# A diagonal of reciprocals as the moving operand of the transposes, in a two-precision attention and feed-forward kernel

## The chip, the cores and the metric

One Trainium2 chip, one core of it. The metric is device time in microseconds (us) of one execution. The kernel before took 974.97 us, the median of 3 runs that lie between 972.93 and 976.83.

## The reference

Windowed attention with global tokens for 4 batches of 8 heads, 512 local and 32 global positions, head dimension 64, then two feed-forward blocks on the 2176 rows of 512 that come out. Cut to what matters:

```
s = concat(scale * q_l @ k_g.T, where(|i - j| <= 32, scale * q_l @ k_l.T, -1e9))
e = exp(s - max(s))
out_l = (e / (sum(e) + 1e-9)) @ concat(v_g, v_l)
out_g = softmax(scale * q_g @ concat(k_g, k_l).T) @ concat(v_g, v_l)
x = rows of (out_g, out_l)
x = (silu(x @ w_gate) * (x @ w_val)) @ w_out          # 512 -> 1536 -> 512
h = x @ w_in                                          # 512 -> 2048 -> 512
y = (max(h, 0) + alpha * min(h, 0)) @ w_out2
```

The changed lines compute `e / (sum(e) + 1e-9)`, in the form that the product with v needs: turned, with the keys on the partitions.

## The kernel before, in words

The feed-forward products are what most of the time goes into. Each weight and each activation is held as a rounded 32-bit value and its rest, and a product is three matmuls (`passes`, line 495: high by high, high by low, low by high). `mm12` (line 502) makes one 128-row piece of a hidden layer from 12 matmuls, `down` the product back to 512 rows. `visit1` is one pass of the first block over some columns of one batch, `visit2` one of the second block.

Attention is cut into units. A `Local` unit is one pair of heads and one half (256) of the positions of one batch, in five steps: `s` (line 164) makes the scores in PSUM (8 matmuls, of which the profile shows two records for each program instruction), masks them and finds the row minimum of the negated scores on VectorE (line 184), and takes the exponential with its row sum on ScalarE (line 197). `n` (line 202) adds 1e-9 to the sums, takes the reciprocals `rc`, and multiplies each of four 128 by 256 blocks of `e` by its column of `rc` (line 207). `t` (line 215) is called twice, once per head: it turns the 128 by 512 probabilities with four TensorE transposes against the identity (line 229) into one PSUM bank, which ScalarE copies to `pt` (line 154). `pv` (line 232) multiplies `pt` with v (line 250) and writes the result to `xa` or `yp`. Batches 2 and 3 (`SPLIT`, line 29) take another way: `n` scales `e` by a power of two as well, and `t` makes two 16-bit parts of it which a DMA turns. Batches 0 and 1 have 16 of the 32 local units, so 64 of the 128 multiplications of line 207 and all 128 transposes of line 229. `Global` units (lines 267 to 336) have steps of the same names and are not touched.

`apump` (line 359) calls one step of three neighbouring units at a time; `pumper` hands such steps out between the pieces of a visit. First come the opening steps of batch 0, with nothing but weight loads beside them (the loop at line 688), then `visit1` runs while the attention of later batches is mixed in. Weights come from DRAM as 64-bit words and are turned to 32 bits on ScalarE and VectorE (`wpump`, line 437) in the same in-order queues. The order on each engine is made when the program is built: the framework's scheduler takes the calls with their priorities and its own estimates of times, so that a change to one step can move others. Buffers of `e`, `pt`, `rc` come from the pool `attp` with two buffers each.

Of the kernel before, what the change touches and what calls it, by code (L numbers as in the profile page):

```python
# [10 lines left out]
F32 = mybir.dt.float32  # L11
# [7 lines left out]
ALU = mybir.AluOpType  # L19
# [8 lines left out]
PSC = 32768.0  # L28
# [14 lines left out]
def kernel(  # L43
# [11 lines left out]
    nc = tc.nc  # L55
# [25 lines left out]
    attp = tc.alloc_tile_pool(name="attp", bufs=2, side="right", reuse_waits="tile")  # L81

    ident = const.tile([128, 128], F32, name="ident")
# [19 lines left out]
    def att_bank():  # L103
        t = att_tags["list"][att_tags["i"] % len(att_tags["list"])]
        att_tags["i"] += 1
        return bank(t)
# [4 lines left out]
    def heat(n):  # L111
        t = bank("g")
        for _ in range(n):
            nc.tensor.matmul(out=t[:, 0:128], lhsT=zero, rhs=zero, start=True, stop=True)
# [35 lines left out]
    def evac(out, in_, name):  # L150
        if frac(name):
            nc.vector.tensor_copy(out, in_)
        else:
            nc.scalar.activation(out=out, in_=in_, func=ACTF.Copy)
# [4 lines left out]
    class Local(Unit):  # L159
# [42 lines left out]
        def n(self):  # L202
            rc = attp.tile([128, 4], F32, tag="rc", name="rc")
            nc.vector.tensor_scalar(out=rc, in0=self.sm, scalar1=1e-9, scalar2=None, op0=ALU.add)
            nc.vector.reciprocal(out=rc, in_=rc)
            for j in range(4):
                nc.vector.tensor_scalar(
                    out=self.e[:, j], in0=self.e[:, j], scalar1=rc[:, j:j + 1],
                    scalar2=PSC if self.split else None, op0=ALU.mult,
                    op1=ALU.mult if self.split else ALU.bypass,  # L210
                )
            if self.split and self.half == 0:
                self.pair.split_v()

        def t(self, h):
            src = self.e[:, 2 * h:2 * h + 2].rearrange("p a b -> p (a b)")
            if self.split:
                if h == 0:
                    self.pt = attp.tile([128, 2, 8, 128], F16, tag="pt", name="pth")
                p = attp.tile([128, 2, 512], F16, tag="p", name="p", bufs=3)  # L220
                nc.scalar.activation(out=p[:, 0], in_=src, func=ACTF.Copy)
                nc.vector.tensor_tensor(out=p[:, 1], in0=src, in1=p[:, 0], op=ALU.subtract)
                nc.sync.dma_start_transpose(out=self.pt[:, h], in_=p.rearrange("p a b -> p (a b)"))
                return
            if h == 0:
                self.pt = attp.tile([128, 2, 512], F32, tag="pt", name="pt")
            t = att_bank()
            for i in range(0, 512, 128):
                nc.tensor.transpose(t[:, i:i + 128], src[:, i:i + 128], ident)  # L229
            evac(self.pt[:, h], t, "cp0" if st["k"] < mark[0] + LAG else "cp1")  # L230

        def pv(self):
# [118 lines left out]
    def later(n, f):  # L351
        due.setdefault(st["k"] + n, []).append(f)
# [72 lines left out]
    def wlow():  # L425
        while wlo and wlo[0][3] <= st["w"] - P["wd"]:
            key, raw, t, _, z = wlo.popleft()
            with pr("hilo"):
                eng = nc.gpsimd if frac("lo" + z) else nc.vector
                eng.tensor_tensor(out=t[:, 1], in0=raw, in1=t[:, 0], op=ALU.subtract)  # L430
            wt[key] = t
            if key[0] == 1:
                i = "gvo".index(key[2])
                with pr("st"):
                    (nc.scalar if P["q_st"] else nc.sync).dma_start(out=w1s[key[1]][:, i], in_=t.bitcast(F32))

    def wpump():
# [21 lines left out]
        for key, raw, pool, _ in ready:  # L459
            t = pool.tile([128, 2, 512], F32R, tag="w", name="w")  # L460
            z = "0" if st["k"] < mark[1] else "1" if st["k"] < mark[2] else "3" if key[0] == 2 else "2"
            with pr("hilo"):
                if frac("hi" + z):
                    nc.vector.tensor_copy(t[:, 0], raw)
                else:
                    nc.scalar.activation(out=t[:, 0], in_=raw, func=ACTF.Copy)
            wlo.append((key, raw, t, st["w"], z))
# [386 lines left out]
```

## Time and profile before

| what | value |
|---|---|
| median of 3 runs | 974.97 us |
| the profiled execution | 976.99 us |
| its span, first to last instruction | 975.2 us |
| mean granted TensorE clock | 0.983 of 2.4 GHz |
| instructions in the trace | 14802 |

The profiled execution is a separate one, 2.0 us above the median of the runs. Its span is 1.8 us shorter than its time; the rest lies around the first and the last instruction. The page of the profile gives busy time of each engine, a picture of the span in 40 slices, the chain of work that ended last, and groups of instructions by line. PE is TensorE's matmuls, PEld its weight loads, DVE is VectorE, ACT is ScalarE. A busy time of PE counts a matmul from its start to its modelled end, and matmuls overlap, so the distance between two starts, and not the duration, is what one of them costs in a row of them.

### The profile page before, as it was taken

The page shows a single profiled execution, that of the slowest core. Times are in us where ns is not written, and L with a number is a line of the kernel's source. Part 1 is how long each engine was busy: PE and PEld are TensorE (multiplying, and loading weights), DVE is VectorE, ACT ScalarE, POOL GpSimd, SP SyncE. Part 2 cuts the span into 40 slices and gives each one's busy share as a digit, 9 for nine tenths or more (in the row PEclk, how much of TensorE's full clock was granted, in tenths as well). Part 3 has the DMA queues.
Part 4 walks back from the last instruction along what each step waited for, and adds up shares of the span by engine and source line. Part 5 has one row for each costly group of instructions (what it writes and reads, how often), then busy time and mean ns, then how long its engine had stood idle before and what let it go on. Part 6 is the DMA issues. An engine that isn't in the chain of part 4 may idle for free.

```text
span 975.2 us, 14802 instructions
## 1 busy us (share of the span) xinstructions
PE 957.0 (98%) x5716; PEld 798.1 (82%) x5716; DVE 553.1 (57%) x1295; ACT 488.7 (50%) x983; POOL 0.7 (0%) x6
## 2 busy tenths in 40 slices
PE   8799999999999999999999999999999999999998
PEld 5577887777777777778999998888888888899897
DVE  5989888774444564426831289834443543544453
ACT  6888999865665666635532256423222322322322
POOL 0000000000000000000000000000000000000000
PEclk7599999999999999999999999999999999999999
DMA  8879795538662466712477043200000100010000
GB/s 263 289 244 333 249 346 183 197 85 238 170 157 73 71 153 172 174 23 87 127 215 221 1 131 115 79 1 21 23 1 0 44 1 1 1 44 1 13 21 22
DMA packets 67478, 111.86 MB, mean 115 GB/s; under 512 B 37712, under 2 KB 41808, under 8 KB 67408
## 3 DMA queue, kind: packets, MB, share of 16 engines
q1 hardware_dynamic: 67408, 110.92, 37.1%
q8 instruction: 45, 0.74, 0.3%
q14 instruction: 25, 0.20, 0.1%
HBM read 79.18 MB, written 23.33 MB: 105 GB/s over the span
## 4 chain that ended last, share of the span: by engine, by line
PE 89%; ACT 5%; DVE 4%; DMA 1%; issue 1%; SPq 1%; ACTq 0%
PE ps_acc L632 19%; PE ps_g L508 18%; PE ps_v L508 18%; PE ps_acc L541 13%; PE ps_a L508 10%; PE ps_a L171 3%; PE ps_a L241 2%; ACT e L197 1%; DMA dbl<-in_w_dram 1%; PE ps_a L250 1%; PE ps_a L282 1%; PE ps_a L229 1%; PE ps_a L325 1%; DVE w L430 1%; PE ps_acc L250 1%
## 5 line engine op out<-in xcount | busy, mean ns | idle before, releaser
L508 PE MATMUL ps_g<-xa,w 128*128 128x512 f32 (+2 forms) x1032 | 209.4, 351 | 0.4 <-ACT sg L555 0.4
L508 PE MATMUL ps_v<-xa,w 128*128 128x512 f32 (+2 forms) x1032 | 207.2, 349 | 0.5 <-DVE w L430 0.5
L508 PEld LDWEIGHTS ps_g<-xa,w 128*128 128x128 f32 x1032 | 169.5, 190 | 29.5 <-issue 7.5
L508 PEld LDWEIGHTS ps_v<-xa,w 128*128 128x128 f32 x1032 | 170.1, 190 | 25.3 <-issue 4.2
L632 PE MATMUL ps_acc<-w,h 128*128 128x512 f32 x561 | 138.3, 392 | 0.0
L632 PEld LDWEIGHTS ps_acc<-w,h 128*128 128x128 f32 x561 | 104.5, 188 | 22.3 <-DVE h L651 0.5
L541 PE MATMUL ps_acc<-h,w 128*128 128x512 f32 (+2 forms) x600 | 119.0, 350 | 0.2 <-DVE h L572 0.2
L541 PEld LDWEIGHTS ps_acc<-h,w 128*128 128x128 f32 x600 | 97.7, 189 | 15.4 <-issue 2.4
L508 PE MATMUL ps_a<-xa,w 128*128 128x512 f32 (+2 forms) x480 | 100.8, 359 | 0.0
L508 PEld LDWEIGHTS ps_a<-xa,w 128*128 128x128 f32 x480 | 83.5, 188 | 13.4
L564 DVE TENSOR_TENSOR t<-ps_v,sg 128x512 f32<-128x512 f32 (+1 forms) x54 | 35.6, 659 | 94.2 <-PE ps_v L508 82.4
L197 ACT ACTIVATE e<-e,mx 128x256 f32<-128x256 f32 x128 | 63.7, 500 | 10.6 <-DVE mx L184 9.7
L650 ACT ACTIVATE h<-g 128x512 fp32r<-128x512 f32 (+2 forms) x55 | 31.2, 568 | 74.4 <-DVE g L649 74.4
L184 DVE CUSTOM_DVE_ANT_0 e<-ps_a,lm 128x256 f32<-128x256 f32 x112 | 41.5, 419 | 44.8 <-PE ps_a L171 44.4
L632 PE MATMUL ps_acc<-w,hx 128*128 128x512 f32 x255 | 63.1, 394 | 0.0
L646 DVE TENSOR_SCALAR g<-ps_a,alpha 128x512 f32<-128x512 f32 (+2 forms) x40 | 26.8, 670 | 57.3 <-ACT r L645 56.8
L632 PEld LDWEIGHTS ps_acc<-w,hx 128*128 128x128 f32 x255 | 47.5, 188 | 10.4
L555 ACT ACTIVATE sg<-ps_g 128x512 f32<-128x512 f32 (+1 forms) x54 | 30.9, 573 | 47.2 <-PE ps_g L508 46.8
L651 DVE TENSOR_TENSOR h<-g,h 128x512 fp32r<-128x512 f32 (+2 forms) x55 | 33.6, 612 | 31.1 <-ACT h L650 31.0
L645 ACT ACTIVATE r<-ps_a 128x512 f32<-128x512 f32 (+2 forms) x40 | 21.2, 530 | 58.7 <-PE ps_a L508 58.3
L649 DVE TENSOR_TENSOR g<-g,r 128x512 f32<-128x512 f32 (+2 forms) x80 | 48.8, 611 | 2.4
L555 ACT ACT_TABLE_LOAD x30 | 38.5, 1283 | 19.4 <-PE ps_g L508 19.0
(133 smaller groups left out, 1124.1 us busy)
## 6 DMA issues: line engine op xcount, KB each, us to landing
w<-w1s SPq DMA_DIRECT2D x54, 512.0 KB, 4.1
dbl<-in_w_dram SPq DMA_DIRECT2D x50, 512.0 KB, 4.0
w1s<-w SPq DMA_DIRECT2D x36, 512.0 KB, 4.9
qk<-in_qk_dram SPq DMA_DIRECT2D x12, 592.0 KB, 5.2
dblx<-in_w_dram SPq DMA_DIRECT2D x9, 512.0 KB, 6.1
yp<-in_w_dram SPq DMA_DIRECT2D x9, 512.0 KB, 5.8
out_dram<-o SPq DMA_DIRECT2D x16, 256.0 KB, 2.1
v<-in_v_dram SPq DMA_DIRECT2D x12, 320.0 KB, 3.7
```

The source lines that it names most:

```text
L171: nc.tensor.matmul(out=s[h][:, 256 * i:256 * i + 256], lhsT=x[rows, WIN + 128 * t:WIN + 128 * t + 128], rhs=x[rows, 128 * t:128 * t + 256] ...
L184: nc.vector.tensor_tensor_reduce(out=self.e[:, j], in0=s[h][:, 256 * i:256 * i + 256], in1=lm[:, 2 * self.half + i], scale=-0.125, scalar= ...
L197: nc.scalar.activation(out=self.e[:, j], in_=self.e[:, j], func=ACTF.Exp, scale=-1.0, bias=mx[:, j:j + 1], accum_out=self.sm[:, j:j + 1],)
L508: nc.tensor.matmul(out=o, lhsT=a, rhs=x, start=(i == 0), stop=(i == 11))
L541: nc.tensor.matmul(out=acc[m][:, 0:n], lhsT=a, rhs=x, start=(f == fs[0] and j == 0), stop=(f == fs[-1] and j == 2),)
L555: nc.scalar.activation(out=sg[:, 0:nn], in_=g[:, 0:nn], func=ACTF.Silu)
L564: nc.vector.tensor_tensor(out=t[:, 0:nn], in0=v[:, 0:nn], in1=sg[:, 0:nn], op=ALU.mult)
L632: nc.tensor.matmul(out=acc[t], lhsT=a, rhs=x, start=(i == 0 and j == 0), stop=(i == NF2 - 1 and j == 2))
L646: nc.vector.tensor_scalar(out=g[:, 0:n], in0=u[:, 0:n], scalar1=0.0, scalar2=alpha[:, f:f + 1], op0=ALU.min, op1=ALU.mult)
L649: nc.vector.tensor_tensor(out=g[:, 0:n], in0=g[:, 0:n], in1=r[:, 0:n], op=ALU.add)
L650: nc.scalar.activation(out=h[:, 0, 0:n], in_=g[:, 0:n], func=ACTF.Copy)
L651: nc.vector.tensor_tensor(out=h[:, 1, 0:n], in0=g[:, 0:n], in1=h[:, 0, 0:n], op=ALU.subtract)
```

## The change

For batches 0 and 1 (units that are not `split`), `n` no longer multiplies `e`. It makes four 128 by 128 tiles `d`, the identity with each row multiplied by that row's reciprocal. `t` multiplies by `d` with ordinary matmuls where it had transposes against the identity: the stationary operand is the same block of `e`, the moving operand is now `d`, and the sum over the rows leaves e turned, with each column already divided. The block of `d` is chosen by head and 128-row tile (`2 * h + i // 2`). The split units keep the old way.

```
@@ n
+            if not self.split:
+                self.d = attp.tile([128, 4, 128], F32, tag="d", name="d")
+                for j in range(4):
+                    nc.vector.tensor_scalar(
+                        out=self.d[:, j], in0=ident, scalar1=rc[:, j:j + 1], scalar2=None, op0=ALU.mult
+                    )
+                return
             for j in range(4):
                 nc.vector.tensor_scalar(
-                    out=self.e[:, j], in0=self.e[:, j], scalar1=rc[:, j:j + 1],
-                    scalar2=PSC if self.split else None, op0=ALU.mult,
-                    op1=ALU.mult if self.split else ALU.bypass,
+                    out=self.e[:, j], in0=self.e[:, j], scalar1=rc[:, j:j + 1], scalar2=PSC, op0=ALU.mult,
+                    op1=ALU.mult,
                 )
@@ t
-            for i in range(0, 512, 128):
-                nc.tensor.transpose(t[:, i:i + 128], src[:, i:i + 128], ident)
+            for i in range(4):
+                nc.tensor.matmul(
+                    out=t[:, 128 * i:128 * i + 128], lhsT=src[:, 128 * i:128 * i + 128],
+                    rhs=self.d[:, 2 * h + i // 2], start=True, stop=True,
+                )
```

The scheduler also orders instructions of the first two batches anew. On TensorE, behind the first scores of batch 0 (`ps_acc_220` and the like are PSUM banks, `qk` holds queries and keys, and line 250 of before is line 259 now, 229 is 235), this stood before:

```order
L171 MATMUL ps_acc_328<-qk 128x256 x2
L229 MATMUL ps_acc_220<-ident,e 128x128 x4
L229 MATMUL ps_acc_233<-ident,e 128x128 x4
L250 MATMUL ps_acc_308<-pt,v 64x256
L171 MATMUL ps_acc_329<-qk 128x256
L229 MATMUL ps_a_280<-ident,e 128x128 x2
L171 MATMUL ps_acc_329<-qk 128x256
L250 MATMUL ps_acc_308<-pt,v 64x256
```

and this stands there now:

```order
L171 MATMUL ps_acc_331<-qk 128x256 x2
L235 MATMUL ps_acc_221<-d,e 128x128 x4
L235 MATMUL ps_acc_234<-d,e 128x128 x4
L235 MATMUL ps_a_282<-d,e 128x128 x4
L259 MATMUL ps_acc_311<-pt,v 64x256
L235 MATMUL ps_a_295<-d,e 128x128 x2
L171 MATMUL ps_acc_332<-qk 128x256 x2
L259 MATMUL ps_acc_311<-pt,v 64x256
```

The first head of the second unit has all its four products ahead of the first unit's product with v; before, it had two behind it, and two further on.

On TensorE just ahead of the first visit's matmuls (line 508 before, 517 now) this stood before:

```order
L250 MATMUL ps_a_509<-pt,v 64x256 x2
L250 MATMUL ps_a_509<-pt,v 64x128 x4
L229 MATMUL ps_v<-ident,e 128x128 x4
L229 MATMUL ps_a_492<-ident,e 128x128 x4
L508 MATMUL ps_v<-xa,w 128x256 x9
```

and now:

```order
L259 MATMUL ps_a_515<-pt,v 64x256 x2
L259 MATMUL ps_a_515<-pt,v 64x128 x4
L235 MATMUL ps_v<-d,e 128x128 x4
L235 MATMUL ps_a_497<-d,e 128x128 x4
L517 MATMUL ps_v<-xa,w 128x256 x6
```

Nothing has moved there but the visit's matmuls, which are broken off after 6 instead of 9 by scores of a global unit. On VectorE, at the second unit's `n` (`raw` and `dbl` are weights on their way to 32 bits), this stood before:

```order
L207 TENSOR_SCALAR e<-e,rc 128x256 x4
L184 ISA e,mx<-ps_g,lm 128x256
L184 ISA mx 128x1
L204 TENSOR_SCALAR rc<-sm 128x4
L184 ISA e,mx<-ps_v,lm 128x256
L184 ISA mx 128x1
L451 TENSOR_SCALAR raw<-raw 128x512
L205 RECIPROCAL rc<-rc 128x4
```

and now:

```order
L209 TENSOR_SCALAR d<-ident,rc 128x128 x4
L204 TENSOR_SCALAR rc<-sm 128x4
L205 RECIPROCAL rc<-rc 128x4
L209 TENSOR_SCALAR d<-ident,rc 128x128
L460 TENSOR_SCALAR raw<-raw 128x512
L209 TENSOR_SCALAR d<-ident,rc 128x128
```

The masking of the fourth unit's scores (`ps_g`, `ps_v`) has gone behind the second unit's diagonals and the first weights. On SyncE's queue some twenty transfers of the first two batches change places with a neighbour; the first of them is a second store of a turned weight (line 435, now 444), which goes ahead of the two loads of queries and keys that stood before it.

## Rows read from the trace of the kernel before

**Rows 1.** The page's picture in 40 slices: TensorE and its granted clock, in tenths.

```profile
PE   8799999999999999999999999999999999999998
...
PEclk7599999999999999999999999999999999999999
```

**Rows 2.** Windows of the whole core: stretch, us, busy us and instructions by engine, clock, DMA.

```profile
0.00:48.00 48.00, 38.14 (x176) 27.37 (x176) 35.30 (x121) 34.83 (x89) 0.70 (x6) 0.68 0.86 276
48.00:140.00 92.00, 88.90 (x751) 75.06 (x751) 80.80 (x224) 84.83 (x176) 0.00 (x0) 1.00 0.83 288
140.00:182.00 42.00, 42.00 (x264) 30.91 (x264) 36.71 (x104) 39.69 (x82) 0.00 (x0) 1.00 0.65 228
...
80.00:100.00 20.00, 19.23 (x168) 16.19 (x168) 19.35 (x59) 18.02 (x40) 0.00 (x0) 1.00 0.93 338
100.00:120.00 20.00, 19.57 (x169) 17.25 (x172) 16.18 (x43) 19.91 (x45) 0.00 (x0) 1.00 0.77 260
```

**Rows 3.** Windows of line 229 alone: stretch, us, PE busy (records), PEld busy, clock, DMA.

```profile
13.90:34.20 20.30, 4.20 (x16) 3.00 (x16) 0.50 0.88 288
34.40:37.70 3.30, 1.09 (x8) 0.86 (x8) 1.00 0.70 250
37.80:47.90 10.10, 1.97 (x8) 1.57 (x8) 0.50 0.88 286
48.00:80.00 32.00, 3.72 (x24) 2.70 (x24) 1.00 0.75 261
80.00:140.00 60.00, 4.63 (x32) 3.68 (x32) 1.00 0.87 302
140.00:182.00 42.00, 4.63 (x32) 3.91 (x32) 1.00 0.65 228
```

**Rows 4.** The chain of waits, 27 to 56 us: start, us, what, count.

```profile
27.83 1.11 PE ps_acc L229 x4
28.95 0.85 PE ps_g L229 x4
...
52.40 0.44 PE ps_a L229 x4
...
53.88 1.43 PE ps_g L508 x12
```

**Rows 5.** Records of line 250: count, duration ns (min/median/max), first and last start, forms.

```profile
L250 PE MATMUL ps_a<-pt,v x156: 272/273/634, 37.6 to 193.6; 128*64 128x128 f32 x104, 128*64 128x256 f32 x52
...
L250 PE MATMUL ps_acc<-pt,v x24: 421/421/687, 14.9 to 32.4; 128*64 128x128 f32 x16, 128*64 128x256 f32 x8
...
L250 PE MATMUL ps_v<-pt,v x12: 421/421/687, 25.0 to 26.5; 128*64 128x128 f32 x8, 128*64 128x256 f32 x4
```

**Rows 6.** Timeline of TensorE at 164 us: start, us, what, count.

```profile
163.86 1.09 PE L250 MATMUL ps_a<-pt,v 128*64 128x256 f32 x12
```

**Rows 7.** Timeline of TensorE, 14 to 42 us; in brackets idle time and its releaser.

```profile
14.87 1.11 PE L250 MATMUL ps_acc<-pt,v 128*64 128x256 f32 x2 [2.47 <-ACT pt L154]
...
37.57 0.98 PE L250 MATMUL ps_a<-pt,v 128*64 128x256 f32 x4 [1.88 <-ACT pt L154]
...
41.91 1.11 PE L229 MATMUL ps_v<-ident,e 128*128 128x128 f32 x4 [2.51 <-DVE e L207]
```

**Rows 8.** Windows of the whole core, by granted clock, at the start.

```profile
13.90:34.20 20.30, 18.43 (x71) 11.64 (x72) 17.06 (x53) 16.19 (x42) 0.00 (x0) 0.50 0.88 288
34.40:37.70 3.30, 1.42 (x12) 1.02 (x12) 2.99 (x9) 3.15 (x9) 0.00 (x0) 1.00 0.70 250
37.80:47.90 10.10, 7.59 (x39) 6.79 (x36) 9.46 (x32) 8.64 (x22) 0.00 (x0) 0.50 0.88 286
```

**Rows 9.** Groups by line and shape on VectorE: busy us, mean ns, idle before.

```profile
L207 DVE TENSOR_SCALAR e<-e,rc 128x256 f32<-128x256 f32 x128 | 36.9, 348 | 0.8
...
L308 DVE TENSOR_SCALAR sg<-sg,rcg 128x640 f32<-128x640 f32 x8 | 4.4, 552 | 0.2
```

**Rows 10.** The chain of waits, at 85 us.

```profile
85.01 0.87 DVE e L207 x3
```

## The prediction

> **What bounds the kernel now.** Read the page's picture first: TensorE is at nine tenths or more from the third slice (24.4 us each) on, but for the last, and its granted clock is full, 2.4 GHz, from the third slice on too [rows 1]. So whatever lengthens TensorE's stream late in the kernel lengthens the kernel, and only the start can hide anything. All changed instructions lie at the start: the 128 transposes of line 229 are at an end by 182 us [rows 3]. So the windows come next [rows 2]. From 140 to 182 us TensorE is busy 42.00 of 42.00 us. From 48 to 140 us it is idle for 3.1 of 92 us, and there VectorE (19.35 of 20 us from 80 on) and ScalarE (19.91 of 20 us from 100 on) are as full as TensorE. Up to 48 us it is idle for 9.9 us. There its clock changes too: the windows by clock [rows 8] show 0.50, that is 1.2 GHz, from 13.9 to 34.2 and from 37.8 to 47.9 us, and full between them, though TensorE was busy only 1.42 of 3.3 us in that stretch. Last comes the chain of waits, which tells where TensorE and where another engine ended last [rows 4, 10].
>
> **TensorE: one more record per turn.** The change replaces 128 transposes (16 units of 8) by 128 ordinary products of 32-bit values. A transpose leaves one record: 8 before 13.9 us and the 120 of the windows [rows 3] make 128. An ordinary 32-bit product leaves two, as line 250 shows: 16 units with 6 products each are 96, and it has 156 + 24 + 12 = 192 records [rows 5]. So 128 records are added, with as many weight loads.
>
> What does one cost? Four transposes at full clock take 0.44 us on the chain, 0.110 us each; four at half clock take 0.85 us, 0.213 us each [rows 4]. The records of line 250 run at the same pace: 12 of them, 4 of them with 256 columns, span 1.09 us [rows 6]. As two heads use 64 columns of the array each, side by side, that is 6 steps for a pair of heads, 2 of which count double, so 8 times 0.110 = 0.88 us and the end of the last record. These have weights of only 64 columns. The nearest row with weights of 128 by 128 that change at each record and a moving operand of similar length is line 508's with 256 columns in its 32-bit form of one record: 12 in 1.43 us, 0.119 us each [rows 4]. I take 0.110, because the new products load the very tile that the transposes load, and keep 0.119 as the upper end. A cost below 0.110 I exclude where the clock is full, since both kinds of 32-bit record already show that pace with nothing to wait for.
>
> The Trainium skill, "TensorE: Matmul & The Clock Gate", section "Terms", says that the transpose mode makes 32-bit matmuls four times faster. By that, a turn would lose a factor of four, not two; the sum would be three times 13.0 us before what is hidden. The rows of line 250 speak for two, so the sum goes by two, and four is a rival below.
>
> **Where the 128 records lie** [rows 3].
> - 140 to 182 us: 32 records, 32 times 0.110 = 3.5 us. TensorE has no idle time there, so all of it is on the path.
> - 48 to 80 us: 24 records, 2.6 us. The chain runs almost wholly on TensorE here [rows 4], so all of it counts.
> - 80 to 140 us: 32 records, 3.5 us. VectorE and ScalarE bind for much of this stretch. Between nothing left of it but 0.4 us (3.5 less the idle 3.1) and all of it, I take half, 1.8 us, because the engines are equally full and neither end is nearer.
> - 13.9 to 34.2 and 37.8 to 47.9 us, at half clock: 16 and 8 records, 24 times 0.213 = 5.1 us. I take it whole: the groups at 27.83, 28.95 and 41.91 us are on the chain, or end a wait of TensorE and have TensorE's own work behind them [rows 4, 7]; the records ahead of 27.83 us I take likewise.
> - The last 16, ahead of 13.9 us and from 34.4 to 37.7 us, at full clock: 1.8 us, costed at nothing. TensorE waits for ScalarE's copy behind each of these two groups, 2.47 us until 14.87 us and 1.88 us until 37.57 us [rows 7], and ScalarE's earlier queue, not the turn, is late there. If that cover is gone, 1.8 us come back.
>
> Sum for TensorE: 3.5 + 2.6 + 1.8 + 5.1 = 13.0 us.
>
> **VectorE: shorter instructions.** 64 multiplications of 128 by 256 at 348 ns become 64 of 128 by 128. Line 308, of the same form on 640 columns, takes 552 ns [rows 9]; (552 - 348) / 384 = 0.53 ns a column, which gives 280 ns for 128 columns, 68 ns less. In all VectorE is relieved of 64 times 68 ns = 4.4 us. Little of that is on the path: TensorE needs the first two diagonals of a head, as it needed the first two blocks. I count 8 instructions, two each ahead of the turns at 27.83 and 41.91 us and the four around 85.01 us [rows 4, 7, 10], so 0.5 us, rounded up to 0.6 for the queue behind them. The upper end is 48 instructions, those of the 12 units ahead of 140 us: 3.3 us. The lower end is nothing.
>
> **Waits, buffers and order.** No wait is new: `d` needs `rc`, which needs the sums of all four exponentials, so `e` is there when `d` is. What goes is that `e` is rewritten before the turn. `d` has two buffers, as `e` has. ScalarE's 32 copies of the turned blocks stay. The scheduler's new order puts the second unit's products ahead of the first unit's product with v, and the masking of the fourth unit's scores behind weights; on SyncE's queue a second store of a turned weight goes ahead of two loads of queries and keys. I cost that at nothing, as the same work stands in the same stretch, with bounds of one wait like that at 41.91 us, 2.5 us [rows 7], either way.
>
> **The sum** is 13.0 - 0.6 = 12.4 us. On the profiled execution, 975.2 us of span in 976.99 us, that is 987.6 us of span and 989.4 us. That execution stands 2.0 us above the median, so against the median the forecast is 974.97 + 12.4 = 987.4 us, 1.3% slower. With the upper ends (0.119 for each record, 1.1 us; the hidden 1.8 and 1.7 us; no help from VectorE, 0.6) it is 992.6 us, with a late wait 995.
>
> **Rivals.**
> 1. **The start hides it all (not slower).** Up to 140 us the chain would run through VectorE and ScalarE, and the added work of TensorE would go into its idle time. The sizes allow it: 9.9 + 3.1 = 13.0 us idle, and 11.2 to 13.0 us added (2.6 + 3.5 + 5.1, and the 1.8 that I costed at nothing). VectorE's 3.3 us would then count in full, against 3.5 us behind 140 us: 975.2 us. It decides once VectorE and ScalarE have their inputs from TensorE at least as long ahead as the added work lasts. For it: 19.35 and 19.91 of 20 us [rows 2]. Against it: the chain on TensorE at 27.83 to 31 and 43 to 80 us, and the idle time lies in single waits. 0.17.
> 2. **The clock rises sooner.** At half clock TensorE is held in two stretches, and both end behind a group of turns [rows 4, 8]. In the second, it works without a pause from 41.91 to 47.9 us before the clock rises. If the denser stream raised it at the second head of each group, at 28.95 and 43.0 us, some 5.2 and 4.9 us of work would take half as long, 5.1 us, and 8 added records would cost 0.110 instead of 0.213, 0.8 us: 981.5 us. Against it: the full clock from 34.4 us on was lost by 37.8 us although 8 turns fell into that stretch [rows 3, 8]; what TensorE does between the turns may decide alone. 0.17. The Trainium skill, same page, section "Part 4: PE-mode transpose", says that a transpose does not count as TensorE being busy for the clock the way a matmul does; by that rule the new products would bring this about. No row here separates the two.
> 3. **A product costs four transposes.** 3 times 13.0 us and the 1.7 us that are then not hidden, less 0.6: 40 us, so 1015 us. The rows of line 250 speak against it. 0.03.
> 4. **The new order opens a wait** in the start, with the upper ends: 993 to 998 us. 0.06.
>
> **How the numbers follow.** The forecast (984 to 993 us) has 0.55, the rivals 0.17, 0.17, 0.03 and 0.06, and 0.02 is left for a gain by the order with the first two rivals together. About 0.5%, 4.9 us, is what a measurement of this kernel can tell from no change, so faster is below 970.1 us, 0.02, and slower is above 979.8 us, 0.81; between lies rival 1 with 0.17. The range from 975 to 995 us takes in half of rival 1, all of rival 2, and the bounds.
>
> **What would show it.** The line of the products should have 256 records and 256 weight loads, spaced at 0.11 us at full clock; four products of one head should take 0.87 us where they took 0.44. TensorE should be without idle time from 140 us on with the same work behind it, and the first block's later visits should start 8 to 13 us later. VectorE's new group should show 64 at about 280 ns, and line 207's successor 64 at 348 ns. The forecast is wrong if the products leave one record each, if the windows up to 140 us show as much idle time gone as work added, or if the clock stands at full before 48 us by more than one stretch.

## The result, and the profile after

The changed kernel takes 986.96 us, the median of 4 runs between 984.7 and 988.32, against 974.17 us for the kernel before in the 4 runs beside it. The ratio is 1.0123, with a 95% interval from 1.0107 to 1.0140: slower by 12.0 us at 975, in an interval of 10.4 to 13.7 us. The prediction was 987.4 us, 12.4 us slower. The profiled execution took 986.79 us, with a span of 984.9 us.

The page of the profile after, TensorE's busy time and the picture in 40 slices of 24.6 us:

```profile
PE 967.8 (98%) x5844; PEld 812.8 (83%) x5844; DVE 549.8 (56%) x1295; ACT 489.4 (50%) x983; POOL 0.7 (0%) x6
...
PE   7999999999999999999989999999999999999998
...
PEclk9999999999999999999999999999999999999999
```

There are 128 more matmul records and 128 more weight loads than before (5844 against 5716 of each), as forecast. TensorE is at nine tenths from the second slice on, but for one slice at eight and the last, and, unlike in [rows 1], the clock stands at nine tenths in the first two slices.

The windows of [rows 2] in the kernel after, and then those of its turns alone (line 235; the columns of [rows 3]):

```profile
0.00:48.00 48.00, 41.39 (x283) 32.35 (x283) 37.37 (x133) 38.08 (x95) 0.70 (x6) 0.96 0.87 291
48.00:140.00 92.00, 89.28 (x735) 78.17 (x734) 79.25 (x215) 84.19 (x174) 0.00 (x0) 0.96 0.85 294
140.00:182.00 42.00, 41.89 (x266) 31.42 (x263) 33.51 (x98) 36.56 (x76) 0.00 (x0) 1.00 0.61 219
182.00:985.00 803.00, 795.26 (x4566) 670.85 (x4565) 399.64 (x851) 330.58 (x640) 0.00 (x0) 1.00 0.27 77
```

```profile
0.00:48.00 48.00, 14.34 (x96) 12.88 (x96) 0.96 0.87 291
48.00:140.00 92.00, 14.08 (x96) 12.97 (x96) 0.96 0.85 294
140.00:182.00 42.00, 6.53 (x48) 6.12 (x48) 1.00 0.61 219
182.00:985.00 803.00, 1.95 (x16) 1.94 (x16) 1.00 0.27 77
```

The records of the turns are 96 + 96 + 48 + 16 = 256. The last 16 of them now lie behind 182 us, so a fixed window no longer holds the same work in both kernels. To see where the time came from, marks that mean the same piece of work are better. I use three, all from the views of single lines: the first matmul of the first visit, the last turn, and the first matmul back to 512 rows of the second block. Each row has count, duration in ns (least, median, most) and the start in us of the first and the last record. The kernel before, lines 508 (first visit), 229 (turns) and 632 (second block):

```profile
L508 PE MATMUL ps_v<-xa,w x1032: 274/386/580, 43.7 to 960.3; 128*128 128x512 f32 x84, 128*128 128x256 f32 x56, 128*128 128x384 f32 x32
```

```profile
L229 PE MATMUL ps_a<-ident,e x100: 270/272/478, 17.1 to 180.9; 128*128 128x128 f32 x100
```

```profile
L632 PE MATMUL ps_acc<-w,h x561: 387/390/499, 601.3 to 969.9; 128*128 128x512 f32 x187
```

The kernel after, where the same lines are 517, 235 and 641:

```profile
L517 PE MATMUL ps_v<-xa,w x1032: 274/385/522, 38.1 to 970.0; 128*128 128x512 f32 x84, 128*128 128x256 f32 x56, 128*128 128x384 f32 x32
```

```profile
L235 PE MATMUL ps_a<-d,e x200: 270/275/580, 13.3 to 186.3; 128*128 128x128 f32 x100
```

```profile
L641 PE MATMUL ps_acc<-w,h x561: 387/390/505, 611.2 to 979.7; 128*128 128x512 f32 x187
```

So the stretch up to the first visit is 5.6 us shorter (43.7 to 38.1), the stretch from there to the last turn 11.0 us longer (137.2 to 148.2), the stretch from the last turn to the second block 4.5 us longer (420.4 to 424.9), and the rest, up to the end of the span, equal (373.9 and 373.7). The sum, rounded, is the 9.7 us between the two spans, 975.2 and 984.9. The middle stretch has the forecast's work; the first and the third are surprises of opposite sign, and the runs below are about them. The medians lie 12.0 us apart, more than these two spans, because the two profiled executions do not stand alike to the runs of their kernels: the one of before was granted 0.983 of the clock over its span, and none of that kernel's other runs whose clock is listed has less.

The price of a record is right. The timeline of TensorE at 165 us, start, length, what, count:

```profile
165.31 1.05 PE L235 MATMUL ps_a<-d,e 128*128 128x128 f32 x8
```

The last of 8 records is 0.275 us long, so 7 steps take 1.05 - 0.275 us, 0.111 us each; the forecast had 0.110. VectorE's instructions have the forecast's length as well, 281 ns against 280 (line 209 makes the diagonals, line 214 divides the rows of batches 2 and 3; mean ns and idle time before):

```profile
L214 DVE TENSOR_SCALAR e<-e,rc 128x256 f32<-128x256 f32 x64 | 18.5, 349 | 0.6
...
L209 DVE TENSOR_SCALAR d<-ident,rc 128x128 f32<-128x128 f32 x64 | 14.4, 281 | 0.4
```

The third stretch has one wait that was not there before. The chain of waits near 500 us:

```profile
491.08 5.32 DMA dbl<-in_w_dram
...
499.16 4.01 DMA dbl<-in_w_dram
...
503.28 0.65 ACT dbl L459
503.94 0.39 ACT sg L564
...
504.37 3.04 PE ps_g L517 x12
```

TensorE waits 2.60 us for the activation `sg`, which stands on ScalarE behind the conversion of a weight (line 459) whose transfer has just landed. TensorE's timeline there, and the group of these matmuls on the page of before and of after, with all idle time ahead of the group at its end:

```profile
504.37 3.04 PE L517 MATMUL ps_g<-xa,w 128*128 128x384 f32 x12 [2.60 <-ACT sg L564]
```

```profile
L508 PE MATMUL ps_g<-xa,w 128*128 128x512 f32 (+2 forms) x1032 | 209.4, 351 | 0.4 <-ACT sg L555 0.4
```

```profile
L517 PE MATMUL ps_g<-xa,w 128*128 128x512 f32 (+2 forms) x1032 | 209.8, 352 | 3.3 <-ACT sg L564 2.6
```

Before, this group waited 0.4 us for `sg` in the whole kernel. Right behind the wait, from 505.8 to 509.2 us, the granted clock is 0.50, which costs about another 1.7 us (an estimate: half of these 3.4 us); this second part is not in the second profile of the change, below.

### The profile page after: what moved, and what is told of

Its sections match the earlier page's. It is cut to its first block, busy times and chain, and to the rows that moved or that the text cites. A ratio compares the mean times of both kernels' runs of the same rounds, so it can differ in the third digit from the quotient of the medians.

```text
span 984.9 us, 15079 instructions
## 1 busy us (share of the span) xinstructions
PE 967.8 (98%) x5844; PEld 812.8 (83%) x5844; DVE 549.8 (56%) x1295; ACT 489.4 (50%) x983; POOL 0.7 (0%) x6
## 4 chain that ended last, share of the span: by engine, by line
PE 88%; DVE 4%; DMA 3%; ACT 3%; issue 1%; SPq 1%; ACTq 0%
PE ps_acc L641 19%; PE ps_g L517 18%; PE ps_v L517 17%; PE ps_acc L550 13%; PE ps_a L517 10%; PE ps_a L171 3%; DMA dbl<-in_w_dram 3%; PE ps_a L235 2%; PE ps_a L250 2%; PE ps_a L259 1%; PE ps_a L334 1%; PE ps_a L291 1%; DVE raw L464 1%; DVE dbl L461 1%; PE ps_a L325 1%
## 5 line engine op out<-in xcount | busy, mean ns | idle before, releaser
L641 PEld LDWEIGHTS ps_acc<-w,hx 128*128 128x128 f32 x255 | 47.5, 188 | 10.4
L564 ACT ACTIVATE sg<-ps_g 128x512 f32<-128x512 f32 (+1 forms) x54 | 31.0, 573 | 45.3 <-PE ps_g L517 44.9
```

What stands on the lines that cost most here:

```text
L564: nc.scalar.activation(out=sg[:, 0:nn], in_=g[:, 0:nn], func=ACTF.Silu)
L641: nc.tensor.matmul(out=acc[t], lhsT=a, rhs=x, start=(i == 0 and j == 0), stop=(i == NF2 - 1 and j == 2))
```

## The experiments

Ratios are to the kernel before, run beside each; a difference in us is the ratio's, at 975 us, unless it is said to be one of medians. Where a stretch is named, it goes by the marks above: to the first visit, to the last turn, to the second block.

**e1: VectorE's relief alone.** The transposes stay, and only half of each block is divided; the other half stays undivided.

```
+                c = 256 if self.split else 128
-                    out=self.e[:, j], in0=self.e[:, j], scalar1=rc[:, j:j + 1],
+                    out=self.e[:, j, 0:c], in0=self.e[:, j, 0:c], scalar1=rc[:, j:j + 1],
```

> Transposes against the identity as before; only 128 of each block's 256 columns are divided by the row total, so part of the result is left undivided. VectorE then has the instruction lengths of the change and TensorE the work of before. Theory A (the second record of each product costs TensorE time, and VectorE's relief is worth little): 972.5 to 974.5 us, granted clock 0.50 in most of 14 to 48 us as before. Rival C (VectorE's relief of 4.4 us counts in full in the start): 970.5 us or less.

Measured: 977.63 us, ratio 1.0008 (0.9995 to 1.0021). VectorE's 4.4 us of relief are worth nothing measurable, and the time lies in neither of the two ranges expected. But its profile, of the quickest of its 12 runs (973.88 us), had the clock of the changed kernel's start, with the transposes in place. The windows of 14 to 38 us (TensorE's clock is the third number from the end), of the kernel before, of the change and of e1:

```profile
14.00:38.00 24.00, 20.35 (x84) 12.88 (x86) 20.45 (x63) 19.74 (x51) 0.00 (x0) 0.57 0.86 282
```

```profile
14.00:38.00 24.00, 19.21 (x127) 14.56 (x128) 22.06 (x74) 22.20 (x57) 0.00 (x0) 0.93 0.87 301
```

```profile
14.00:38.00 24.00, 16.59 (x97) 10.46 (x96) 22.70 (x76) 22.61 (x60) 0.00 (x0) 0.93 0.89 306
```

```profile
L509 PE MATMUL ps_v<-xa,w x1032: 274/374/562, 37.8 to 956.6; 128*128 128x512 f32 x84, 128*128 128x256 f32 x56, 128*128 128x384 f32 x32
```

The first visit begins at 37.8 us in e1, as early as in the change. So it does not take the products to have the clock up.

**a2, a3 and a1: second profiles** of the kernel before, of e1 and of the change, without an edit.

> The kernel before itself, for a second profile. If the clock between 14 and 48 us is a matter of the single execution, this profile has another pattern than the first (26 us at half clock ahead of the first visit at 43.7 us); with 10 us or less at half clock the first visit starts at 38 to 41 us, and the rest of the kernel is as long as in the first profile within 2 us. If the pattern belongs to the kernel, it comes again. Time as before within 0.3%.

> The kernel of e1 (part of the rows undivided), for a second profile. Its first one had 3.4 us at half clock ahead of the first visit and was the quickest of its 12 runs. If the clock goes by the execution, this one has more half clock and a later first visit, 40 to 45 us; if by the kernel, 37 to 39 us again. Time 974 to 978 us, as before.

> The changed kernel itself, a second profile and more times. If the full clock between 11 and 48 us in its first profile belongs to the change, this profile shows it again. If it is a matter of the single execution, the granted clock in the first 50 us differs from the first profile, and with it the start of the first visit (38 us at full clock, 43 us or later with some 20 us at half clock). Time 984 to 989 us either way; a wait near 500 us for a weight that is there again belongs to the kernel.

Measured: a2 975.42 us, ratio 0.9997 (0.9983 to 1.0011); a3 975.02 us, 1.0005 (0.9982 to 1.0028); a1 987.52 us, 1.0123 (1.0100 to 1.0147). In a2 the clock had another pattern than in the first profile of the very same kernel, 0.77 from 14 to 38 us where it had 0.57, and the first visit began at 41.2 us instead of 43.7:

```profile
14.00:38.00 24.00, 17.66 (x92) 11.57 (x92) 22.59 (x68) 22.09 (x57) 0.00 (x0) 0.77 0.93 311
```

```profile
L508 PE MATMUL ps_v<-xa,w x1032: 277/386/582, 41.2 to 957.1; 128*128 128x512 f32 x84, 128*128 128x256 f32 x56, 128*128 128x384 f32 x32
```

a3 stood at 0.79 and began the first visit at 39.4 us, e1 at 0.93 and 37.8 us. So the clock of the start goes by the execution, and no single profile tells what a kernel has there. a1 has 0.86 and 39.1 us, later than the change's first profile by 1 us. Its wait near 500 us is there again, 2.57 us, without the fall of the clock behind it, and its span is 981.8 us. The wait belongs to the changed kernel; the clock behind it doesn't.

**e2: the products alone.** Rows are divided as before, and the turn is an ordinary product with the identity.

```
-                nc.tensor.transpose(t[:, i:i + 128], src[:, i:i + 128], ident)
+                nc.tensor.matmul(
+                    out=t[:, i:i + 128], lhsT=src[:, i:i + 128], rhs=ident, start=True, stop=True
+                )
```

> Rows divided on VectorE as before, and the turn made by ordinary products with the identity. Theory A: 256 records for the turns, spaced 0.12 us at full clock, the start at full clock as in the changed kernel, 986 to 989 us. Rival B (the time of the change comes from the new order and its late wait for a weight near 500 us): more than 3 us away from the changed kernel's 987 us, and no idle time of TensorE near 500 us.

**e3: the transposes twice.** The same number of records, of the other kind.

```
-                nc.tensor.transpose(t[:, i:i + 128], src[:, i:i + 128], ident)
+                for _ in range(2):
+                    nc.tensor.transpose(t[:, i:i + 128], src[:, i:i + 128], ident)
```

> Rows divided as before, and each transpose made twice into the same place, so 256 records of the transpose kind spaced 0.11 us. If the density of TensorE's stream decides about the clock in the start: full clock in most of 14 to 48 us, first visit near 38 us, 983 to 986 us. If the kind of instruction decides (a transpose does not count): 0.50 in most of 14 to 48 us as before, first visit at 46 us or later, 987 to 991 us.

Measured: e2 986.39 us, 1.0101 (1.0079 to 1.0123); e3 985.86 us, 1.0091 (1.0070 to 1.0112). The two are alike: 256 records for the turns, the same order of TensorE's instructions ahead of the first visit, and the clock in the start at 0.79 and 0.72. So an ordinary product costs what two transposes cost. The windows of 14 to 38 us, e2 first:

```profile
14.00:38.00 24.00, 19.10 (x99) 13.53 (x100) 20.59 (x65) 18.26 (x47) 0.00 (x0) 0.79 0.90 307
```

```profile
14.00:38.00 24.00, 19.15 (x95) 13.45 (x96) 20.26 (x65) 17.92 (x45) 0.00 (x0) 0.72 0.90 301
```

The first visit begins at 45.3 and 46.0 us, 4 to 5 us later than in a2, whose clock was much the same (0.77). That is near the forecast's 5.1 us for the start. It is not the records alone: the scheduler has ordered the start of e2 and e3 anew, the same way in both and neither as before nor as in the change, and both profiles are of the slowest of six runs (988.84 and 988.62 us). The expectation that the clock would tell the kinds apart failed both ways: it was neither as in the first profile of the change nor as in the first of before.

**e4 and e5: the change in the first five units alone, and in all but these.** The five are those whose turns lie ahead of the first visit.

```
+            self.diag = pair.b == 0 and (half == 0 or pair.p == 0)                                   # e4
+            self.diag = not self.split and not (pair.b == 0 and (half == 0 or pair.p == 0))          # e5
-            if not self.split:
+            if self.diag:
...
+                if not self.diag:
+                    nc.tensor.transpose(t[:, 128 * i:128 * i + 128], src[:, 128 * i:128 * i + 128], ident)
+                    continue
```

> Diagonals and ordinary products in the first five local units alone, those ahead of the first visit; the other eleven divide rows and transpose as before. Theory A: 80 product records with the start at full clock, first visit near 38 us instead of 43.7 us, and 88 transposes at 0.11 us later: 974.2 less 5.6, so 968 to 970.5 us. Rival D (the early start is given back between 60 and 140 us, where VectorE and ScalarE bind): 973 to 976 us.

> The complement of e4: row division and transposes in the first five local units, diagonals and products in the other eleven. Theory A: 88 added records, 0.09 to 0.12 us each, on the path: 7.7 to 10 us over before. Rival B (the gap comes from the order and waits that the first units' change makes): under 5 us over before.

Measured: e4 979.5 us, 1.0044 (1.0023 to 1.0064), so 4.3 us slower with 40 added records; e5 982.25 us, 1.0072 (1.0052 to 1.0092), so 7.0 us slower with 88. By the prediction's terms, e4 is 5.1 and e5 is 3.5 + 2.6 + 1.8 = 7.9 us, each less about 0.3 of help from VectorE. The two add up to 11.3 us, and the change has 12.0. Both theories as I had stated them for e4, with a gain from the clock, were wrong: there was none (0.57 from 14 to 38 us, first visit at 43.2 us).

Ahead of the first visit e4 runs the instructions of the change, in the change's order on TensorE, VectorE, ScalarE and SyncE's queue, and e5 those of the kernel before. So each is one more profile of the same start under another clock. The windows of 14 to 38 us and the first visit's matmuls, of e4 and then of e5:

```profile
14.00:38.00 24.00, 21.38 (x91) 14.74 (x92) 19.16 (x63) 19.00 (x49) 0.00 (x0) 0.57 0.79 261
```

```profile
L522 PE MATMUL ps_v<-xa,w x1032: 277/364/501, 43.2 to 962.8; 128*128 128x512 f32 x84, 128*128 128x256 f32 x56, 128*128 128x384 f32 x32
```

```profile
14.00:38.00 24.00, 17.29 (x90) 10.79 (x90) 22.61 (x71) 21.33 (x56) 0.00 (x0) 0.71 0.89 308
```

```profile
L522 PE MATMUL ps_v<-xa,w x1032: 277/374/581, 40.7 to 963.7; 128*128 128x512 f32 x84, 128*128 128x256 f32 x56, 128*128 128x384 f32 x32
```

| granted clock, 14 to 38 us | first visit with the change's start (us) | with the start of before (us) |
|---|---|---|
| 0.93 | 38.1 (after) | |
| 0.86 | 39.1 (a1) | |
| 0.77 | | 41.2 (a2) |
| 0.71 | | 40.7 (e5) |
| 0.57 | 43.2 (e4) | 43.7 (before) |

The first visit goes by the clock, whichever of the two kernels it is.

**e6, e7 and e8: the clock held up by other work.** Small 16-bit products of zeros stand ahead of the first turn and ahead of the product with v in the first five units, in the kernel before (e6: 8 of them, e8: 4) and in the change (e7: 8).

```
+        def warm(self, t):
+            if self.pair.b == 0 and (self.half == 0 or self.pair.p == 0):
+                for _ in range(8):
+                    nc.tensor.matmul(out=t[:, 0:128], lhsT=zero, rhs=zero, start=True, stop=True)
...
+            if h == 0:
+                self.warm(t)
...
             o = att_bank()
+            self.warm(o)
```

> The kernel before, with 8 small 16-bit products of zeros ahead of the first turn and ahead of the product with v of each of the first five units, into a PSUM bank that is overwritten behind them. If the clock in the start is lost to TensorE's pauses, these fill them: full clock in most of the first 48 us, first visit at 38 us, and 970 to 973 us. If the clock doesn't follow them, or they cost what they give, 975 to 979 us.

> The changed kernel with the same small products. At full clock in both, the difference from e6 is free of the clock's state: theory A has 10 to 13 us between them, of which under 1 us lies ahead of the first visit. If the early products cost what the prediction gave them at half clock, the first visit starts 2 to 5 us later than in e6.

> As e6, with 4 small products in each place instead of 8. If what they cost in TensorE's time weighs as much as the clock they keep, this is quicker than e6: 970 to 973 us. If 4 are too few to hold the clock, 974 to 977 us, with 10 us or more at half clock ahead of the first visit.

Measured: e6 973.36 us, 0.9977 (0.9958 to 0.9995); e7 984.47 us, 1.0095 (1.0072 to 1.0117); e8 979.29 us, 1.0030 (1.0013 to 1.0047). e7 had the full clock all through the start, and its first visit began at 38.9 us; e6 had 0.86 from 14 to 38 us, and began it at 41.7. Between the two lie 11.1 us by the medians: with the clock up in both, the change costs about what it costs without. e6 is the quickest kernel of this study, by 2.2 us in an interval from 0.5 to 4.1. The clock that each run lists for its whole span goes with that: the median is 0.994 in e6's 12 runs against 0.988 in the 17 of before beside them. Among the 78 runs of before beside the experiments, 0.001 more of the clock goes with 0.5 us less of time, so 0.006 would be about 3 us, an estimate from these runs. e8's runs were granted 0.989, as those of before beside them: half the number of small products did not keep the clock up. Why e8 is then 2.9 us slower than without any is not shown.

**e9: a third landing buffer** for the weights of the second block in the change, in the place that the attention's buffers leave.

```
+        if i == 2 and third_dbl:
+            return third_dbl[0].tile([128, 512], I64, tag="dblz", name="dblz")
         return dblp.tile([128, 512], I64, tag="dbl", name="dbl")
```

> The changed kernel with a third landing buffer for the weights of the second block, in the place that the attention buffers leave free; all of TensorE's order up to there is the same. If the wait near 500 us in both profiles of the change comes from the two landing buffers and from transfers that land a microsecond later, it goes: no idle time of TensorE over 0.7 us between 440 and 520 us, and 1.008 to 1.010 of the time before, 2 to 4 us less than the change. If the wait has another cause, it stays at 2 to 3 us and the time at 1.011 to 1.014.

Measured: 991.59 us, 1.0172 (1.0146 to 1.0199), slower than the change and outside both expected ranges, and the wait is still there, in a profile of the quickest of the five runs (986.86 us). ScalarE's and TensorE's timelines at 500 us, with idle time and its releaser in brackets:

```profile
501.40 0.65 ACT L462 ACTIVATE dblz<-dblz 128x512 int32<-128x512 uint32 x1 [2.23 <-DMA dblz<-in_w_dram]
501.96 0.47 ACT L567 ACTIVATE sg<-ps_g 128x384 f32<-128x384 f32 x1
```

```profile
502.48 3.91 PE L520 MATMUL ps_g<-xa,w 128*128 128x384 f32 x12 [3.10 <-ACT sg L567]
```

So a third landing buffer does not take the wait away. With it, ScalarE's queue still holds the activation behind a conversion that waits for a transfer, and TensorE waits 3.10 us.

## Why the prediction came out right, and where its steps did not

**Two records for one** held: 5844 records, and 0.111 us for each at full clock, against 0.110. The upper price of 0.119, from line 508, was not needed. e3 has the same price from the other side: two transposes for each one cost 8.9 us, the products of e2 9.9. The rival of four transposes for a product is out. The sentence of the Trainium skill ("TensorE: Matmul & The Clock Gate", "Terms") on a fourfold gain of the transpose mode does not describe this kernel, where the factor was two.

**From the first visit to the last turn** lie 3.5 + 2.6 + 1.8 us of the forecast, less about 0.3 of VectorE's: 7.6. The means of the two profiles of each kernel give 147.0 us (148.2 and 145.8) against 136.7 us (137.2 and 136.2), 10.3 us more. The term that was too small is the middle one, of which I hid half in VectorE's and ScalarE's work: with all of it on the path it is 9.3 us. e2 and e3 have 145.5 and 145.2 us in this stretch, 8.7 us more than before. So in these kernels the added records were not hidden between 80 and 140 us, although VectorE and ScalarE looked as full as TensorE. e5 is less plain: all its 88 added records lie behind its first visit, and the stretch is 142.4 us there, 5.7 us more. Rival 1, that the start hides it all, is out.

**Up to the first visit** the forecast was 5.1 us more for TensorE and about 0.3 less for VectorE. The change's two profiles have 38.1 and 39.1 us there, the two of before 43.7 and 41.2: 3.9 us less. This is the step that failed, by its place. The table of e4 and e5 shows what the 3.9 us are: most of it is the clock of these four executions. Where the change's start and that of before both had 0.57, their first visits lie 0.5 us apart, and the six points together leave no more than about 1 us between the two starts at one clock (an estimate from these six). So at one clock the forecast's 5.1 us do not show in the change.

They do show when the rows are divided as before: e2 and e3, at 0.79 and 0.72, begin the first visit 4 to 5 us later than a2 at 0.77, though in an order of their own. Two readings are left, and no run tells them apart: the shorter instructions and the order of the change make up for some 5 us, where the forecast gave them 0.6 us and nothing; or part of the 4 to 5 us belongs to the order of e2 and e3. With transposes, the shorter instructions and their order are worth less: e1 begins the first visit at 37.8 us where the change at the same clock has 38.1, a3 at 39.4 us (0.79) where a2 has 41.2 (0.77). And e1 and a3 as a whole are not quicker (1.0008 and 1.0005). On the mean of two profiles each, their first visit is 3.9 us earlier than before, their last turn 3.5, their second block 1.7 and their end 1.2: half is given back between the last turn and the second block, which are 422.4 us apart there, against 420.6. Of that, 1.2 and 1.6 us are one wait of TensorE for ScalarE at 188 and 190 us, which the profiles of before and of the change don't have.

**From the last turn to the second block** the forecast had nothing. The change has 424.9 and 423.0 us there, before 420.4 and 420.9: 3.3 us more. 2.6 us of it is the wait near 500 us, which both profiles of the change show, and e7 (1.88 us) and e9 (3.10 us) too. In e2 to e5 it is 0.7 to 1.2 us, and in neither profile of before is there one over 0.7. Its last link is shown (a conversion on ScalarE behind a late transfer, ahead of the activation that TensorE needs). From 200 us on TensorE, VectorE, ScalarE and SyncE's queue have the same instructions in the same order as before, so the wait does not come from a new order there. What differs is the length of transfers: two of the loads ahead of that conversion, the same two in both profiles of the change, took 5.2 to 5.8 us from issue to landing (one is the 5.32 us at 491.08 in the chain above), and 3.8 to 4.6 us in both profiles of before. What lengthens them, when all of the edits are 300 us past, is not settled; a third buffer does not take the wait away (e9).

**The clock rival** had 0.17. What it describes was in the first profile (0.93 in place of 0.57), and yet the time came out where the forecast without it lay. The rival's cause is out: e4 runs the change's start, products and order, at 0.57, e1 has 0.93 with transposes alone, and e3 with twice the transposes has nearly the clock of e2 with products. For the same reason the prediction's sign of being wrong by the clock (full before 48 us by more than one stretch) does not tell the kernel: the change's first profile shows it, e4 does not. The rule of the Trainium skill ("TensorE: Matmul & The Clock Gate", "Part 4: PE-mode transpose") that a transpose does not count for the clock as a matmul does finds no support in these pairs, in which other matmuls stand between the turns.

So the total was right partly because errors cancelled. At one clock, the forecast had about 5 us too much up to the first visit, against 3 us too little up to the last turn and 3 us in a wait that it didn't have. The profiles alone do not add up to the measured 12.0 us: on two profiles each, the three stretches give -3.9 + 10.3 + 3.3 = 9.7 us. The clock that the runs list can account for the rest. Over the whole span, the two profiles of before were granted 0.983 and 0.991, where the median of its 78 runs beside the experiments is 0.989; the two of the change had 0.992 and 0.995, where the median of its 10 runs is 0.991. So the profiles lie 0.0065 apart and the runs 0.002. Among the runs of before 0.001 goes with 0.5 us, among those of the change with 0.9, so the 0.0045 between are worth 2 to 4 us, an estimate from these runs; 2.3 us are missing.

What makes the total more than luck is the price of the records: e2 and e3, with rows divided as before and 128 records more of either kind, cost 9.9 and 8.9 us, and e4 and e5 take 4.3 and 7.0 us for the two halves of the change, where the terms gave 4.8 and 7.6. e4 and e5 bear out the sums and not the places: in e4's profile the first visit is only 0.7 us later than on the mean of the two of before, and the stretch behind it 1.7 us longer, though no record was added there.

## What to carry to other kernels

A turn by an ordinary 32-bit product cost TensorE two records of 0.111 us where a transpose cost one of 0.110, however cheap the division became that it replaces; where TensorE is the engine that is never idle, look for the work to save there, and leave the division on the engine with room. When an engine is busy for 97% of a stretch and three engines look equally full, count added work on the one that stays full afterwards in whole, with part of it as the lower end (here 88 records, 9.7 us, came out as 10.3, 8.7 and 5.7 us). And where a start runs at a changing clock, take several profiles before reading a cause from one of them, look for runs of another kernel that have the same instructions up to there, and compare the clock of the profiled execution with that of the other runs.

## What the runs showed of the hardware that was not expected

The same kernel was granted 0.57 of the clock from 14 to 38 us in one execution and 0.77 in another, and its first visit moved by 2.5 us with it; the change's start had 0.93 and, in e4, 0.57, and its first visit moved by 5.1 us. Ordinary 32-bit products load their 128 by 128 weights in 192 ns (median) where transposes of the same tile load them in 141 ns, yet the spacing of the matmuls is nearly the same, 0.111 against 0.110 us. Work that is added only ahead of 190 us was followed by a wait of 2.6 us near 500 us, in both profiles of the change.
